# Stores of left and right output columns: from POOL's queue and whole row groups to SyncE's queue and row halves

## The chip, the cores and the metric

The kernel runs on one core of a Trainium2 chip. The metric is the device time of one execution in microseconds (us), the median of the runs; less is better.

## The reference

Two stages, the second fed by the first. Attention: batch 4, 8 heads, 768 positions, head size 64. Heads flagged as retrieval heads look back over all positions, the others over the first 4 positions and a window of 64. The result is laid out as `x` with 3072 rows and 512 columns. Then a soft mixture of experts with 8 experts and 4 slots for each:

```python
logits = x @ phi                      # 3072 x 32
slot_input = softmax over rows (logits).T @ x       # 32 x 512
for e in range(8):                    # 4 slots each
    h = relu(slot_input[e] @ w1[e])   # 512 -> 1024
    slot_out[e] = h @ w2[e]           # 1024 -> 512
out = softmax over slots (logits) @ slot_out        # 3072 x 512, float32
```

The output is 6.29 MB in float32. The weights `w1` and `w2` are 16.8 MB each in float32 and are stored as bf16 on the chip.

## The kernel before

A planner (`Plan`) takes a list of operations with costs and keys and writes out an order for all engines before the program is built; the key decides among operations that could start. `pl.op` adds one.

All weights but one half are loaded by POOL's queue (`dma`, line 347), one after the other, over the whole run. The last experts' `w2` comes in column halves: experts 6 and 7 (`NSPLIT = 2`), left 256 columns first, then the right 256 columns. `load_half(15, 1)` is the last load; it lands in `qk`.

The end of the kernel, which the change touches, goes like this. `w2_op` (line 1046) multiplies one expert's hidden rows by its `w2`, in the left columns (`c = 0`) and then the right ones (`c = 1`). Between the last two experts of each half stands `wait_zeros` (ops `ZT0` and `ZT1`, line 1064): multiplications of a tile of zeros, on PE, whose results nobody reads. `emit_so` (line 1104) scales the half of the slot outputs.

The output rows are six groups of 512 rows (`gi` 0 to 5); a group is a tile of 128 partitions with four rows `r` each. `out_tile` (lines 1121, 1129, 1131) multiplies one row `r` of a group by the slot outputs on PE, and ACT or DVE scale it into the group's buffer. Groups 0 to 2 (`NL = 12` rows, the list `halved`) are done in two passes, left 256 columns and right 256 columns, so that the left pass can go ahead of the last weight half. Groups 3 to 5 are done in full rows after it.

`store` (line 1140) writes rows `r0` to `r1` of a group to the output, from POOL's queue or from SyncE's. It waits for the scaling of these rows. Left stores: group 0 in rows 0 and 1 to 3, groups 1 and 2 whole, all from POOL. Right stores: group 0 in rows 0 to 1 and 2 to 3, groups 1 and 2 whole, all from SyncE. Full rows: three stores of 1 MB from SyncE. SyncE's queue also carries three loads at the program's start (lines 475 to 477), so that it issues ten transfers. A queue's instructions are issued in order; each one's wait holds up those behind it. Each transfer has a semaphore out of eight per kind of queue, so that from the ninth on it also waits for the landing of the one eight before it.

Of the kernel before, what the change touches and what calls it, by code (L numbers as in the profile page):

```python
# [151 lines left out]
def pe(ns, n=1):  # L152
    occ = ns * n / 1000.0
    return {"PE": (occ, occ + 0.27)}
# [72 lines left out]
def kernel(  # L227
# [101 lines left out]
    def on(eng, occ, late=0.18):  # L329
        return {eng: (occ, occ + late)}  # L330
# [349 lines left out]
    for b in range(B):  # L680
# [57 lines left out]
        for ns in ([(0, 1), (2, 3)] if b == 0 else [(0, 1, 2, 3)]):  # L738
# [10 lines left out]
            def emit_ex2(o, b=b, sc=sc, ns=ns):  # L749
# [4 lines left out]
            e = pl.op(f"EXX.{b}.{ns[0]}", on("ACT", 0.12 + 0.213 * len(ns)), key - 1.0, deps=[a, PTXb[b].op],  # L754
                      acq=[PTXb[b]] if ns[0] == 0 else [], rel=[sc], emit=emit_ex2)

            def emit_mx(o, b=b, ns=ns):
# [4 lines left out]
            e = pl.op(f"MX.{b}.{ns[0]}", on("DVE", 0.07 + 0.134 * len(ns)), key + 0.3, deps=[e] + [o_hm[n] for n in ns],  # L762
                      emit=emit_mx)
# [209 lines left out]
    kt = T * 16 + 10  # L973
# [65 lines left out]
    w2o = {}  # L1039

    def w2_op(e, c0, c1):
        def emit_w2(o):
            e4, g0 = e // 4, e % 4
            for fo in range(8):
                g = fo % 4
                nc.tensor.matmul(banks[so.slot][32 * g:32 * (g + 1), 256 * c0:256 * c1],
                                 hT_t[e4][:, fo, 32 * g0:32 * (g0 + 1)], w_row(NE + e, fo) if c1 - c0 == 2 else w_half(NE + e, c0)[:, fo, :],
                                 start=(e == 0 and fo < 4), stop=(e == NE - 1 and fo >= 4),
                                 tile_position=(0, 32 * g), skip_group_check=True)

        land = [wland[NE + e]] if c1 - c0 == 2 else [hland[NE + e, c0]]
        o = pl.op(f"W2.{e}" + ("" if c1 - c0 == 2 else f".{c0}"), on("PE", 0.22 * (c1 - c0), 0.27),
                  kt + (29 + e if c0 == 1 else 16 + e),
                  deps=[hte[e // 4]] + land + [w2o[c] for c in range(c0, c1) if c in w2o],
                  acq=[so] if e == 0 else [], emit=emit_w2, mode="c32", mm=8)
        for c in range(c0, c1):
            w2o[c] = o
# [3 lines left out]
    def wait_zeros(name, n, key, dep, first=False):  # L1061
        def emit_z(o):
            for _ in range(n):
                nc.tensor.matmul(banks[zw.slot][:, 0:448], ident, zt, start=True, stop=True)

        pl.op(name, pe(190, n), key, deps=[dep], acq=[zw] if first else [], rel=[zw], emit=emit_z, mode="full", mm=n)
# [4 lines left out]
    for c in range(2):  # L1071
        for e in range(NE - NSPLIT, NE):
            w2_op(e, c, c + 1)
            if e == NE - 2:
                wait_zeros(f"ZT{c}", 3, kt + (29.5 + e if c else 22.5), w2o[c], c == 0)

    def out_lhs(gi, r):
        return expT[:, r, 128 * gi:128 * (gi + 1)]
# [32 lines left out]
    def ot_view(gi):  # L1111
        return slots[wbuf[gi].slot][:, 0:8 * KB].bitcast(F32).rearrange("p (r d) -> p r d", r=4)
# [3 lines left out]
    def out_tile(m, gi, r, c0, c1, key):  # L1116
        bf, w = Buf("BK"), 256 * (c1 - c0)
        cs = slice(256 * c0, 256 * c1)

        def emit_om(o):  # L1120
            nc.tensor.matmul(banks[bf.slot][:, 0:w], out_lhs(gi, r), slot_out[:, cs], start=True, stop=True)  # L1121

        a = pl.op(f"OM.{gi}.{r}.{c0}", on("PE", 0.06 + w / 2400.0, 0.27), key, deps=so_e[c0:c1], acq=[bf],
                  emit=emit_om, mode="full", mm=1)

        def emit_oe(o):
            d, sc_ = ot_view(gi)[:, r, cs], rrow[:, 4 * gi + r:4 * gi + r + 1]
            if o.eng == "ACT":
                nc.scalar.activation(d, banks[bf.slot][:, 0:w], ACT.Copy, scale=sc_)  # L1129
            else:  # L1130
                nc.vector.tensor_scalar(d, banks[bf.slot][:, 0:w], sc_, None, op0=ALU.mult)  # L1131

        x, y = (0.24 + w / 1070.0, 0.13 + w / 960.0)
        oe[m, gi, r] = pl.op(f"OE.{gi}.{r}.{c0}", {"ACT": (x, x + 0.19), "DVE": (y, y + 0.17)}, key, deps=[a, o_rw[gi]],
                             rel=[bf], emit=emit_oe)

    def store(eng, m, gi, r0, r1, cs, key):
        def emit_st(o):
            dst = out[512 * gi:512 * (gi + 1), :].rearrange("(p r) d -> p r d", r=4)
            (nc.gpsimd if eng == "POOL" else nc.sync).dma_start(dst[:, r0:r1, cs], ot_view(gi)[:, r0:r1, cs])  # L1140

        pl.op(f"ST.{m}.{gi}.{r0}", on(eng, 0.7), key, deps=[oe[m, gi, r] for r in range(r0, r1)], emit=emit_st)

    NL = 12
    halved = [(gi, min(4, NL - 4 * gi)) for gi in range((NL + 3) // 4)]
    for gi, n in halved:
        for r in range(n):
            out_tile("l", gi, r, 0, 1, kt + 30 + 0.1 * (4 * gi + r))
    for gi, r0, r1 in [(0, 0, 1), (0, 1, 4)] + [(gi, 0, n) for gi, n in halved[1:]]:
        store("POOL", "l", gi, r0, r1, slice(0, 256), kt + 31 + gi + 0.1 * r0)  # L1150
    for gi, n in halved:
        for r in range(n):
            out_tile("r", gi, r, 1, 2, kt + 40 + 0.1 * (4 * gi + r))
        for r0, r1 in [(0, 2), (2, 4)] if gi == 0 else [(0, n)]:
            store("SP", "r", gi, r0, r1, slice(256, 512), kt + 41 + gi + 0.1 * r0)
    for gi in range(6):
        n = dict(halved).get(gi, 0)
# [55 lines left out]
```

## Time and profile before

| | |
|---|---|
| median of 3 runs | 148.62 us (148.15 to 148.8) |
| the profiled execution | 148.91 us, span 147.1 us |
| granted TensorE clock, mean | 0.968 |
| busy share of the span | PE 81%, DVE 75%, ACT 73%, POOL 29% |
| DMA packets | 33.40 MB, mean 227 GB/s |
| read from HBM, written to it | 52.49 MB, 6.29 MB |

Times in the profile count from the span's start. A row of the timeline is start, length, engine, line, operation, and what is written and read; an "x2" merges two neighbours. A row of a DMA window gives a queue's packets, its MB and the share of 16 engines' time that its packets took; packets may overlap, so that a share can be above one. `q0 software_dynamic` holds what POOL issues, `q1 hardware_dynamic` what SyncE issues. Loads that convert float32 to bf16 count by what they write, half of what they read.

### The profile page before, as it was taken

To read this page: it belongs to the slowest core of one execution; us is meant where nothing else is said; L and a number is where in the kernel's file an instruction comes from. 1 tells how busy PE (TensorE), PEld (TensorE's weight loads), DVE (VectorE), ACT (ScalarE), POOL (GpSimd) and SP (SyncE) were. 2 spreads that over 40 slices of the span, in tenths; PEclk is the share of its full clock that TensorE was granted. 3 is DMA by queue.
4 is the path that set the end of the run, shared out by engine and by line. 5 is a ranking of instruction groups with operands and counts; after the bars stand their busy time and mean duration, and the time that the engine had idled before them with its cause. 6 is when DMAs were issued, how large, how long until landed. Compare 5 with 4: busy or idle time off the path is not lost.

```text
span 147.1 us, 4879 instructions
## 1 busy us (share of the span) xinstructions
PE 119.7 (81%) x2107; PEld 79.2 (54%) x2107; DVE 111.0 (75%) x254; ACT 107.9 (73%) x147; POOL 42.0 (29%) x75
## 2 busy tenths in 40 slices
PE   0167988999989999999999999999959899879000
PEld 0045666677776657776558766666745445443000
DVE  1786299999999999999799899999973312549500
ACT  3152689999999997999998999999971460649200
POOL 6988631120311380100170011405380000340000
PEclk9999999999999999999999999999995999999965
DMA  5999999999999999999999999999999999989995
GB/s 147 270 207 212 217 213 214 213 215 211 216 215 214 212 215 214 217 214 214 215 215 217 214 215 214 214 214 215 214 214 214 206 196 197 168 309 347 404 423 212
DMA packets 13815, 33.40 MB, mean 227 GB/s; under 512 B 802, under 2 KB 6562, under 8 KB 13282
## 3 DMA queue, kind: packets, MB, share of 16 engines
q0 software_dynamic: 11472, 27.27, 94.1%
q1 hardware_dynamic: 2322, 5.83, 10.5%
q8 instruction: 16, 0.26, 0.6%
q14 instruction: 5, 0.04, 0.1%
HBM read 52.49 MB, written 6.29 MB: 400 GB/s over the span
## 4 chain that ended last, share of the span: by engine, by line
PE 27%; DVE 26%; DMA 18%; ACT 15%; issue 5%; POOL 1%; SPq 0%; DVEq 0%; ACTq 0%; POOLq 0%
DMA qk<-in_moe_w_dram 14%; ACT pt L726 11%; PE sc L656 6%; DVE pt L672 5%; PE pv L800 5%; DVE xv L824 5%; DMA phf<-in_moe_phi_dram 4%; DVE qk L336 4%; PE tr L604 3%; PE tr L630 3%; PE bk L1121 2%; PE tr L863 2%; DVE xv L336 2%; DVE slot L1131 2%; DVE vf L705 2%
## 5 line engine op out<-in xcount | busy, mean ns | idle before, releaser
L726 ACT ACTIVATE pt<-sc 128x1024 bf16<-128x1024 f32 x80 | 77.0, 1047 | 3.0 <-PE sc L656 2.8
L656 PE MATMUL sc<-qk 64*128 64x512 bf16 (+3 forms) x256 | 31.4, 311 | 1.2 <-ACT pt L726 0.8
L672 DVE TENSOR_TENSOR pt<-pt,msk 128x1024 bf16<-128x1024 bf16 (+1 forms) x48 | 29.0, 610 | 2.0 <-ACT pt L726 1.8
L800 PEld LDWEIGHTS <-pt 128*128 128x128 bf16 x640 | 23.4, 98 | 6.2 <-issue 5.2
L800 PE MATMUL pv<-vx,pt 128*128 128x65 bf16 x320 | 25.6, 193 | 0.3 <-DVE xv L824 0.2
L800 PE MATMUL pv<-vf,pt 128*128 128x65 bf16 x320 | 21.3, 195 | 0.9 <-DVE xv L824 0.9
L347 POOL DMA_DIRECT2D slot<-in_moe_w_dram x11 | 7.7, 696 | 40.0 <-PE tr L630 34.3
L336 DVE COPY qk<-tr 128x768 bf16<-128x768 bf16 (+2 forms) x33 | 15.1, 482 | 2.1 <-PE tr L604 1.8
L630 PE MATMUL tr<-ident,slot 128*64 128x128 bf16 (+1 forms) x448 | 16.3, 219 | 0.4 <-ACT qk L334 0.3
L824 DVE TENSOR_TENSOR xv<-pv,rs 128x768 bf16<-128x768 f32 (+1 forms) x17 | 15.5, 911 | 0.6
L630 PEld LDWEIGHTS <-slot 128*64 128x64 bf16 (+1 forms) x448 | 13.1, 109 | 5.1 <-issue 4.8
L656 PEld LDWEIGHTS <-qk 64*128 64x128 bf16 x256 | 10.4, 94 | 9.6 <-issue 3.3
L887 POOL COPY expT<-eT 128x192 bf16<-128x192 bf16 x12 | 7.4, 667 | 12.5 <-ACT eT L870 12.5
L1131 DVE TENSOR_SCALAR slot<-bk,rrow 128x256 f32<-128x256 f32 (+1 forms) x19 | 9.2, 562 | 2.2 <-PE bk L1121 2.2
L336 DVE COPY xv<-tr 128x512 bf16<-128x512 bf16 (+2 forms) x20 | 8.0, 410 | 2.5 <-PE tr L604 2.2
L836 PE MATMUL tr<-ident,xv 128*128 128x128 bf16 x96 | 8.4, 224 | 1.3 <-DVE xv L824 0.9
L604 PEld LDWEIGHTS <-slot 96*64 96x64 bf16 x192 | 6.8, 141 | 4.3 <-issue 4.0
L604 PE MATMUL tr<-ident_u,slot 96*64 96x96 bf16 x192 | 7.9, 248 | 1.6 <-DVE phi L544 1.1
L336 DVE COPY xT<-tr 128x768 bf16<-128x768 bf16 (+1 forms) x14 | 7.5, 539 | 1.1 <-PE tr L836 1.1
L1129 ACT ACTIVATE slot<-bk,rrow 128x256 f32<-128x256 f32 (+1 forms) x17 | 7.7, 570 | 0.9 <-PE bk L1121 0.9
L690 PE MATMUL tr<-ident,xv 128*128 128x128 bf16 x96 | 8.1, 220 | 0.0
L1140 POOL DMA_DIRECT2D out_dram<-slot x4 | 2.9, 714 | 17.7 <-DVE slot L1131 17.6
(121 smaller groups left out, 165.6 us busy)
## 6 DMA issues: line engine op xcount, KB each, us to landing
slot<-in_moe_w_dram POOLq DMA_DIRECT2D x10, 1024.0 KB, 24.6
out_dram<-slot SPq DMA_DIRECT2D x3, 1024.0 KB, 5.9
slot<-in_q_dram POOLq DMA_DIRECT2D x2, 768.0 KB, 19.9
slot<-in_k_dram POOLq DMA_DIRECT2D x2, 768.0 KB, 23.8
qk<-in_moe_w_dram SPq DMA_DIRECT2D x1, 1024.0 KB, 6.3
slot<-in_v_dram POOLq DMA_DIRECT2D x2, 512.0 KB, 21.5
qk<-in_moe_w_dram POOLq DMA_DIRECT2D x1, 1024.0 KB, 17.4
vx<-in_moe_w_dram POOLq DMA_DIRECT2D x1, 1024.0 KB, 21.5
```

The source lines that it names most:

```text
L336: nc.vector.tensor_copy(dst, src)
L347: acq=[buf] if buf else [], lead=1.3, emit=lambda o: nc.gpsimd.dma_start(dst(), src))
L604: nc.tensor.transpose(t[64 * i:64 * (i + 1), :, :, s, :], rv[:, i, 8 * c + s, :], ident_u)
L630: nc.tensor.transpose(t[64 * i:64 * (i + 1), :, s, :], rv[:, i, 8 * c + s, :], ident[0:R, 0:R])
L656: nc.tensor.matmul(scb[sc.slot][:, i, c:c + 128 * nb], kk, qq.rearrange("p b c -> p (b c)"), start=True, stop=True)
L672: nc.vector.tensor_tensor(pT, pT, mh, op=ALU.mult)
L690: nc.tensor.transpose(t[:, 128 * j:128 * (j + 1)], vT[:, 6 * n + j, :], ident)
L726: nc.scalar.activation(pTs[PTb[b, n].slot][:, :, 512 * g:512 * (g + 1)], scb[sc.slot], ACT.Exp, scale=scale)
L800: nc.tensor.matmul(pvb[:, bk, c:c + 65], lt, rhs, start=(j == 0), stop=(j == i))
L824: nc.vector.tensor_tensor(xo, pvw[:, :, :, 0:64], r.rearrange("p i (j o) -> p i j o", o=1).to_broadcast([P, 2, i1 - i0, 64]), op=ALU.mult)
L836: nc.tensor.transpose(t[:, 128 * i:128 * (i + 1)], xv[:, i, 128 * n:128 * (n + 1)], ident)
L1131: nc.vector.tensor_scalar(d, banks[bf.slot][:, 0:w], sc_, None, op0=ALU.mult)
```

## The change

The left stores of groups 1 and 2 move from POOL's queue to SyncE's, and each becomes two stores of two rows. The right stores of groups 1 and 2 also become two stores of two rows each. SyncE issues sixteen transfers instead of ten. The left stores come ahead of the right ones on that queue. Group 0's stores and the full rows are as before. `ZT1`, the zeros ahead of the right half's last expert, has two multiplications instead of three; `ZT0` keeps three.

```diff
@@ weights w2, by halves @@
             if e == NE - 2:
-                wait_zeros(f"ZT{c}", 3, kt + (29.5 + e if c else 22.5), w2o[c], c == 0)
+                wait_zeros(f"ZT{c}", 2 if c else 3, kt + (29.5 + e if c else 22.5), w2o[c], c == 0)
@@ stores @@
-    for gi, r0, r1 in [(0, 0, 1), (0, 1, 4)] + [(gi, 0, n) for gi, n in halved[1:]]:
-        store("POOL", "l", gi, r0, r1, slice(0, 256), kt + 31 + gi + 0.1 * r0)
+    for gi, r0, r1 in [(0, 0, 1), (0, 1, 4)] + [(gi, x, x + 2) for gi, n in halved[1:] for x in (0, 2)]:
+        store("SP" if gi else "POOL", "l", gi, r0, r1, slice(0, 256), kt + 31 + gi + 0.1 * r0)
     for gi, n in halved:
         for r in range(n):
             out_tile("r", gi, r, 1, 2, kt + 40 + 0.1 * (4 * gi + r))
-        for r0, r1 in [(0, 2), (2, 4)] if gi == 0 else [(0, n)]:
+        for r0, r1 in [(0, 2), (2, 4)]:
             store("SP", "r", gi, r0, r1, slice(256, 512), kt + 41 + gi + 0.1 * r0)
```

## The prediction

> **What bounds the kernel now.** I read the page first, for the span and the DMA rows.
>
> ```profile
> span 147.1 us, 4879 instructions
> DMA  5999999999999999999999999999999999989995
> q0 software_dynamic: 11472, 27.27, 94.1%
> q1 hardware_dynamic: 2322, 5.83, 10.5%
> ```
>
> The DMA engines are busy in nearly every slice, to the last one. Transfers issued by POOL run on q0, those issued by SyncE on q1. Next I read the stretch that the change touches, with the table of busy time by stretch (columns: PE, PEld, DVE, ACT, POOL, granted clock, DMA share, GB/s).
>
> ```profile
> 120.00:125.00 5.00, 5.00 (x90) 2.40 (x83) 1.31 (x3) 0.69 (x1) 0.00 (x0) 1.00 1.45 195
> 127.50:128.00 0.50, 0.47 (x4) 0.28 (x3) 0.50 (x2) 0.50 (x3) 0.45 (x1) 1.00 0.72 93
> 129.00:129.50 0.50, 0.30 (x2) 0.09 (x1) 0.04 (x1) 0.00 (x1) 0.50 (x1) 1.00 0.40 127
> 129.50:130.00 0.50, 0.00 (x0) 0.00 (x0) 0.00 (x0) 0.00 (x0) 0.49 (x2) 1.00 0.96 334
> 130.50:131.00 0.50, 0.43 (x16) 0.36 (x13) 0.03 (x1) 0.41 (x1) 0.00 (x0) 1.00 0.66 246
> 131.00:131.50 0.50, 0.38 (x4) 0.34 (x4) 0.28 (x2) 0.07 (x1) 0.00 (x0) 1.00 1.00 393
> ```
>
> From 131.0 us on the DMA engines are full and stores are all that runs on them; before that lie two thin places, 129.0 to 129.5 (share 0.40) and 130.5 to 131.0 (0.66). Then the chain of waits, from 108.94 on (start, length, what), which says when the right half can begin:
>
> ```profile
> 108.94 21.16 DMA qk<-in_moe_w_dram
> 130.15 0.43 PE bk L1046 x8
> 130.59 0.48 ACT msk L1104
> 131.12 1.61 PE bk L1121 x12
> ```
>
> The last weight half lands at 130.10 (108.94 + 21.16), and only then can the right columns be multiplied and scaled. Last, the timeline of POOL and of SyncE's queue shows where the stores are issued (start, length):
>
> ```profile
> 127.37 0.58 POOL L1140 DMA_DIRECT2D out_dram<-slot  x1 [17.56 <-DVE slot L1131]
> 128.05 0.76 POOL L1140 DMA_DIRECT2D out_dram<-slot  x1
> 128.81 1.52 POOL L1140 DMA_DIRECT2D out_dram<-slot  x2
> 132.09 0.41 SPq L1140 DMA_DIRECT2D out_dram<-slot  x1
> 132.60 0.45 SPq L1140 DMA_DIRECT2D out_dram<-slot  x1
> 133.54 0.62 SPq L1140 DMA_DIRECT2D out_dram<-slot  x1
> 134.32 0.53 SPq L1140 DMA_DIRECT2D out_dram<-slot  x1
> 135.65 0.35 SPq L1140 DMA_DIRECT2D out_dram<-slot  x1
> ```
>
> So the question about the end is what the slowest DMA engine still has to move. The DMA windows (packets, MB, share of 16 engines) answer it:
>
> ```profile
> DMA packets 6, 0.00 MB, mean 12 GB/s; under 512 B 0, under 2 KB 6, under 8 KB 6
> q0 software_dynamic: 6, 0.00, 9.0%
> DMA packets 69, 0.27 MB, mean 338 GB/s; under 512 B 2, under 2 KB 3, under 8 KB 69
> q0 software_dynamic: 29, 0.12, 97.1%
> q1 hardware_dynamic: 54, 0.06, 74.4%
> q0 software_dynamic: 17, 0.00, 8.6%
> ```
>
> The first two rows are 129.10 to 129.35: six packets, a share of 9.0%. While all engines read weights the share was 1.45 (row 120 to 125), so 9.0% is 0.062 of that, one engine in sixteen: fifteen engines stand idle and one still reads the last weight half. The third row is 129.7 to 130.5, where one data packet under 2 KB is left (two of the three are semaphore writes under 512 B): that engine reads until about 129.7. The fourth row is 133.15 to 133.50, stores of q0 alone; the last two are 133.50 to 133.74, where q1 takes over as q0 runs out, the last engine near 133.7.
>
> **The change part by part.** Same bytes, same packets of rows; different queue, size and issue time. The rates come from three windows: q0 stores at 131.0 to 133.4, the two half stores of right group 0 on q1 at 133.74 to 135.1, the whole stores of right groups 1 and 2 on q1 at 135.25 to 137.75.
>
> ```profile
> DMA packets 241, 0.92 MB, mean 382 GB/s; under 512 B 17, under 2 KB 17, under 8 KB 241
> DMA packets 486, 0.47 MB, mean 348 GB/s; under 512 B 24, under 2 KB 486, under 8 KB 486
> DMA packets 934, 0.94 MB, mean 376 GB/s; under 512 B 16, under 2 KB 934, under 8 KB 934
> ```
>
> Left groups 1 and 2, 1.049 MB: at q0's 382 GB/s they take 2.75 us. As four halves on q1 no row shows them on the left, but the right halves of group 0 have the very shape: at 348 GB/s 3.01 us, +0.27. The other bound is the rate of whole q1 stores, 376 GB/s: 2.79 us, +0.04.
>
> Right groups 1 and 2, again 1.049 MB: now 2.79 us at 376 GB/s, as halves 3.01 us at 348, +0.22; the other bound is 0. Together +0.04 to +0.49. The rows that are nearest, same queue and same shape, stand at the upper end; but that window begins while q0 is only just empty and some of its slowness may be that, so I take +0.4.
>
> The gaps. With POOL, left groups 1 and 2 are issued at 128.81 and after it, since one issue takes about 0.76 us of the engine. The scaling shows when the rows were ready:
>
> ```profile
> 127.00 2.04 DVE L1131 TENSOR_SCALAR slot<-bk,rrow 128x256 f32<-128x256 f32 x5
> 127.07 1.93 ACT L1129 ACTIVATE slot<-bk,rrow 128x256 f32<-128x256 f32 x5
> ```
>
> The engines take turns on rows, a pair every 0.39 us, and the last two pairs are group 2's, ending near 128.65 and 129.04; group 1's end near 127.91 and 128.27. SyncE can then issue at about 128.05, 128.5, 129.0 and 129.5 instead of 128.81 and 129.57. The delay from an issue on SyncE to its first packet is seen at the program's start:
>
> ```profile
> 0.73 0.38 SPq L475 DMA_DIRECT2D qk<-in_moe_w_dram  x1
> DMA packets 0, 0.00 MB, mean 0 GB/s; under 512 B 0, under 2 KB 0, under 8 KB 0
> q1 hardware_dynamic: 9, 0.07, 150.0%
> ```
>
> No packet from 0.73 to 1.75, nine from 1.7 to 2.0: about 1.03 us. The left halves reach the engines from 129.1 on and the thin places fill up. For fifteen engines the left half ends earlier, but the right half can't begin before 132.09 + 1.03 = 133.12, where it now begins at 133.50: at most 0.38 us. For the sixteenth there is nothing to fill. It has read until 129.7 and then owes 98 KB of left stores (a sixteenth of 1.573 MB); at 382/16 = 23.9 GB/s that is 4.1 us, which ends at 133.8, where q0 does run out. It has no idle time now, so it ends no earlier. That these two are the same engine I infer from the sum, as no view numbers the engines. The kernel waits for the last engine, so I take 0 for the gaps and keep -0.38 as the bound.
>
> Issues on SyncE: six more of 0.41 to 0.62 us each. Four lie between 128.05 and 130, when its queue is empty until 132.09. Two more lie between 132.60 and 135.65: at 0.5 us apiece the six of the right side end near 135.1, before the whole rows are ready at 135.65. The last half of group 2 goes out at about 134.65, 0.33 us later than the whole at 134.32, but it stands behind five halves of 0.75 us that begin near 133.8, so its turn comes after 137. Nothing waits behind it. POOL loses two issues and has no work after them. Each store from SyncE's ninth transfer on waits for the landing of the one eight before; the tightest is the first right half of group 2, behind a left half that is over 2 us old. All this is free as long as the stores queue at the engines; without that cover the 0.33 us would show.
>
> One zero multiplication less in ZT1:
>
> ```profile
> 128.56 0.74 PE L1064 MATMUL bk<-zt,ident 128*128 128x448 bf16 x3
> 130.15 0.40 PE L1046 MATMUL bk<-qk,xT 128*32 128x256 bf16 x8 [0.84 <-DMA qk<-in_moe_w_dram]
> ```
>
> PE then idles about 1.04 us before the last weight half instead of 0.84; the wait is for the DMA, so 0. If the granted clock fell to half for it, the right matmuls (12 in 1.61 us by the chain, 0.13 a row) would take 0.27 us a row against 0.20 for DVE and ACT together (two rows every 0.39 us), and the first right store would come some 0.3 us later, at 133.4 on the engines and so inside the last one's backlog: 0 again.
>
> The Trainium skill's page "DMA: Bandwidth & Descriptors" (Rules for kernel authors) speaks against cutting transfers: coalesce small ones, and two halves of one transfer only run one after the other on the same engines. Its fit (Anatomy of one DMA) is 2.0 us fixed plus bytes, so six more transfers would cost 12 us if they ran strictly one by one; the rows above, a mean of 348 against 376 GB/s, show the fixed part overlapped and only a twelfth of the rate lost.
>
> **Sum.** 0.27 + 0.22, taken as +0.4, gaps 0, rest 0. The profiled execution took 148.91 us, 0.29 above the median of 148.62. 148.91 + 0.4 = 149.31 in its terms, 149.0 us against the median. Its own range is 148.7 to 149.2.
>
> **Rivals.** First, the gaps pay. If it is not one engine that sets the end, but all sixteen in turn, the right half starts 0.38 us earlier and the halves run at 376 GB/s: 148.62 - 0.38 + 0.04 = 148.3 us. For it speaks the empty row of 129.10 to 129.35; against it the sum that leads the slow engine to 133.8.
>
> Second, slower: the left halves push the last weight half back. They reach the slow engine near 129.1, when it has some 17 weight packets left (six in 0.25 us until 129.7). Now q0 keeps stores behind weights; on q1 they may be taken in turns. A 1 KB store packet takes 47 ns of an engine (348/16 = 21.8 GB/s). One per weight packet delays the landing by 0.8 us, and the right half comes at 133.9 instead of 133.12, still behind the left stores, which end near 134 on that engine: free. From two per weight packet on it decides: 1.6 us, the right half comes at 134.7, some 0.7 us after the slow engine ran dry, with the halves' 0.49: 148.62 + 1.2 = 149.8 us. Against it speaks the only other place where both queues hold work, 4.95 to 5.25:
>
> ```profile
> q1 hardware_dynamic: 70, 0.05, 52.1%
> q0 software_dynamic: 8, 0.02, 44.5%
> ```
>
> There q0 begins as q1 empties, and at 133.5 q1 begins as q0 empties although the store had been issued 1.4 us before: both look like one queue run out before the other is taken, though neither proves it. The same page (Queues, rings and completion order) says otherwise: each engine goes round between the queues, packet groups of some 9 to 17 descriptors at a time. By that rule this rival holds.
>
> Third, the cut transfers cost nothing at 376 GB/s and the gaps nothing either: 148.7, inside the forecast's range. That the edits are not made can be left out: the four left halves and four right ones stand on SyncE's queue in the changed program.
>
> **How the numbers follow.** About 0.5%, 0.74 us, is what a measurement of this kernel can tell from no change, so 147.88 and 149.36 are the borders. Forecast 0.5, of which 0.09 spills over 149.36 (all the upper costs and a little more); gaps pay 0.2, of which 0.05 falls below 147.88; weights pushed back 0.2, slower; something not seen 0.1, of which 0.02 faster, 0.06 slower. Faster 0.07, same 0.58, slower 0.35. The range goes from the first rival's 148.3 less 0.1 to the second's 149.8 plus 0.2.
>
> **What would show it.** Right: q1 packets from about 129.1 on, the window at 129.2 no longer empty, the last weight half still landing near 130.1, the right stores' rate near 348 GB/s throughout, the whole rows' stores ending some 0.4 us later. Wrong: a landing of the last weight half beyond 130.8, or q1 empty at 133 to 134 (second rival); the last store ending before 145.2 (first rival).

## Result: 0.36% faster, and most of it after the last store

| | before | after |
|---|---|---|
| median, 22 runs each | 148.43 us | 147.81 us |
| lowest to highest | 147.75 to 148.95 | 147.30 to 148.44 |
| ratio, 95% interval | | 0.9964 (0.9949 to 0.9978) |
| profiled execution, span | 148.91, 147.1 | 148.12, 146.3 |

The change gains 0.36% of 148.43, 0.53 us by the ratio; the medians themselves lie 0.62 us apart. The gain is inside the 0.5% that the prediction called no change, but the interval excludes 1, the sign is against the +0.4 us that was forecast, and 147.81 lies below the forecast's own range (148.7 to 149.2) and below that of all rivals together (148.2 to 150.0). The kernel before took 148.43 us here instead of the 148.62 that the prediction started from, so that 0.2 us of the distance is its starting point.

The profile after, the rows that answer to those of before. First the table of busy time by stretch (PE, PEld, DVE, ACT, POOL, granted clock, DMA share, GB/s):

```profile
129.00:129.50 0.50, 0.18 (x5) 0.17 (x8) 0.03 (x1) 0.00 (x0) 0.00 (x0) 1.00 1.01 354
130.50:131.00 0.50, 0.50 (x6) 0.45 (x5) 0.29 (x1) 0.18 (x1) 0.00 (x0) 1.00 1.06 371
131.00:131.50 0.50, 0.50 (x6) 0.43 (x5) 0.50 (x2) 0.50 (x2) 0.00 (x0) 1.00 0.92 311
```

The two thin places of before (shares 0.40 and 0.66) are full in this execution. Then the timeline of SyncE's queue and of PE, and the chain:

```profile
127.94 0.40 SPq L1140 DMA_DIRECT2D out_dram<-slot  x1
128.44 0.45 SPq L1140 DMA_DIRECT2D out_dram<-slot  x1
128.99 0.45 SPq L1140 DMA_DIRECT2D out_dram<-slot  x1
129.53 0.45 SPq L1140 DMA_DIRECT2D out_dram<-slot  x1
129.43 0.40 PE L1046 MATMUL bk<-qk,xT 128*32 128x256 bf16 x8 [0.32 <-DMA qk<-in_moe_w_dram]
109.49 19.89 DMA qk<-in_moe_w_dram
```

The four left halves go out as early as was said. The last weight half lands at 129.38 (109.49 + 19.89) instead of 130.10, and PE waits only 0.32 us for it. Whether the change did that is a question for the experiments.

The row that matters most stands behind the last store. These are SyncE's own instructions from the last DMA packet to the end, in the view of line 1208 (count, shortest/median/longest ns, first and last start); before first, after second:

```profile
L1208 SPq EVENT_SEMAPHORE  x9: 17/28/28, 145.8 to 147.0; - x9
```

```profile
L1208 SPq EVENT_SEMAPHORE  x3: 17/17/28, 145.4 to 146.2; - x3
```

At its end the program waits for every DMA semaphore in a fixed row; in the trace one instruction starts some 0.06 us after the other. The semaphores of SyncE's transfers are taken in turn, eight of them. In both views the first instruction is the wait for the last store itself, and the last two belong to the closing barrier. With ten transfers the last store has the second semaphore: when it lands, six more instructions follow whose semaphores are long there. With sixteen transfers the last store has the eighth, and nothing follows but the barrier. From the last packet to the end of the span, the tail, the kernel before takes 1.62 us (145.48 to 147.10), the changed one 1.27 (145.04 to 146.31).

### The profile page after: what moved, and what is told of

Read it like the earlier page. It is cut to its first block, busy times and chain, and to the rows that moved or that the text cites. A ratio compares the mean times of both kernels' runs of the same rounds, so it can differ in the third digit from the quotient of the medians.

```text
span 146.3 us, 4885 instructions
## 1 busy us (share of the span) xinstructions
PE 120.2 (82%) x2106; PEld 79.2 (54%) x2106; DVE 110.5 (76%) x254; ACT 108.2 (74%) x147; POOL 40.4 (28%) x73
## 4 chain that ended last, share of the span: by engine, by line
PE 31%; DVE 26%; DMA 18%; ACT 12%; issue 5%; POOL 1%; SPq 0%; DVEq 0%; ACTq 0%; POOLq 0%
DMA qk<-in_moe_w_dram 14%; ACT pt L726 9%; PE sc L656 7%; DVE pt L672 5%; PE pv L800 5%; DVE xv L824 5%; PE tr L604 5%; DMA phf<-in_moe_phi_dram 4%; DVE qk L336 3%; PE tr L630 3%; PE bk L1121 3%; PE tr L690 2%; DVE xv L336 2%; PE tr L863 2%; PE tr L836 2%
## 5 line engine op out<-in xcount | busy, mean ns | idle before, releaser
L836 PE MATMUL tr<-ident,xv 128*128 128x128 bf16 x96 | 8.3, 219 | 1.7 <-DVE xv L824 0.9
L690 PE MATMUL tr<-ident,xv 128*128 128x128 bf16 x96 | 8.8, 232 | 0.0
L836 PEld LDWEIGHTS <-xv 128*128 128x128 bf16 x96 | 5.9, 97 | 3.2 <-DVE xv L824 1.8
```

What stands on the lines that cost most here:

```text
L690: nc.tensor.transpose(t[:, 128 * j:128 * (j + 1)], vT[:, 6 * n + j, :], ident)
L836: nc.tensor.transpose(t[:, 128 * i:128 * (i + 1)], xv[:, i, 128 * n:128 * (n + 1)], ident)
```

## Experiments

Theory 1: the six waits at the program's end, the exit, are most of the gain, 0.35 us. Theory 2: most of it comes from the stores, by filled gaps. Spare loads of 64 bytes at the program's start set the count of SyncE's transfers without touching a store.

**The exit alone, three times.** The kernel before and

```diff
-        nc.sync.dma_start(phf, ...)
+        nc.sync.dma_start(phf, ...); [nc.sync.dma_start(spare[:, x_, :], ri_src) for x_ in range(6)]
```

> The kernel before, with six loads of 64 bytes more at the start of SyncE's queue into a spare tile, so that it issues sixteen transfers, the stores as before. Theory 1 (the exit): the last store's semaphore is then the last of the row of waits at the end instead of the third, and the six waits of 0.06 us behind it are already passed; 0.37 us less, ratio 0.9975 to the kernel before, and the profile's tail from the last landing to the end 0.87 us instead of 1.23. Theory 2 (the stores): the gain of the change comes from filled gaps and earlier stores, which this kernel doesn't have; ratio 1.000.

> The kernel before with six small loads once more, for the size of the stores' own part beside the next one: 0.9975 by the exit's waits alone.

> The kernel before with six small loads: the exit's waits alone, 0.35 us, ratio 0.9976.

Measured: 0.9975 (0.9961 to 0.9990), 0.9993 (0.9967 to 1.0018), 0.9963 (0.9938 to 0.9987); the mean is 0.9977, 0.34 us. The second interval alone doesn't exclude 1. The end of the first, in the same view:

```profile
L1208 SPq EVENT_SEMAPHORE  x3: 17/17/28, 145.3 to 146.1; - x3
```

Three instructions as in the changed kernel; the tail is 1.26 to 1.27 us in the three traces. (The expectations' 1.23 and 0.87 us count from the end of the wait for the last store, 0.38 to 0.40 us behind the last packet; the difference is the same.) Six loads that nobody reads are worth over half of the change.

**Halfway.** The same with `range(3)`, so that the last store has the fifth semaphore.

> The kernel before with three small loads: thirteen transfers, the last store's semaphore in the middle of the row. Theory 1: three waits are left behind the last landing instead of six or none, the tail from the last packet to the end halfway between 1.62 and 1.27 us, 1.44. If the tail does not go by this row, it stays at 1.62.

```profile
L1208 SPq EVENT_SEMAPHORE  x6: 17/28/28, 144.6 to 145.6; - x6
```

Six instructions, a tail of 1.45 us, against 1.62 with nine and 1.27 with three: 0.06 us for each wait that stands behind the last landing. Its single time, 147.47 us, says nothing by itself. Over all fourteen kept traces the tail goes by the count of transfers alone: 1.61 to 1.62 us with ten or eighteen (three traces), 1.45 with thirteen, 1.25 to 1.27 with sixteen (ten traces), whatever the stores are.

**The changed kernel without the exit's gain, twice.** The change and `range(2)`: eighteen transfers, the last store has the second semaphore again.

> The changed kernel with two loads of 64 bytes more at the start of SyncE's queue, so that the last store takes the same semaphore as in the kernel before. Theory 1 (the exit): the six waits come back, 0.37 us more than the changed kernel; what is left is the stores' own part, ratio about 0.9989 to the kernel before, tail 1.23 us. Theory 2 (the stores): the ratio stays at 0.9964.

> The changed kernel with two small loads, so that its last store has the same semaphore as in the kernel before: what differs from the kernel before is the stores' own part alone. If that part is about 0.18 us, as the runs so far have it, ratio 0.9988; if there is none, 1.000.

Measured: 0.9981 (0.9963 to 1.0000) and 0.9988 (0.9961 to 1.0016). Its end is that of before:

```profile
L1208 SPq EVENT_SEMAPHORE  x9: 17/28/28, 145.3 to 146.5; - x9
```

The tail is 1.62 us. So the stores' own part, the gain that doesn't come from the exit, is what is left, 0.0015 on the mean or 0.2 us, and neither interval by itself proves it.

**The change itself once more.**

> The changed kernel itself on the same chip: exit's waits 0.35 us and stores' own part 0.18 us, ratio 0.9964.

0.9965 (0.9941 to 0.9990), as the first time.

**Left move alone, right halves alone.** Each with spare loads up to sixteen transfers and three multiplications in `ZT1`. The left move alone, twice (right groups 1 and 2 whole):

```diff
-        for r0, r1 in [(0, 2), (2, 4)]:
+        for r0, r1 in [(0, 2), (2, 4)] if gi == 0 else [(0, n)]:
```

> The left move alone, in halves on SyncE; right groups whole, three multiplications in ZT1, two small loads so that SyncE issues sixteen transfers. Theory 1: the exit's 0.37 us and the stores' own part, ratio about 0.9964. Theory 2: the left move carries all, 0.9964 too. By the term of the prediction that right halves cost 0.22 us it would be 0.995; if they cost nothing, 0.9964.

> The left move alone at sixteen transfers once more. If the stores' own part is real, the ratio is 0.0010 to 0.0015 below that of the kernel before with six small loads; if it is chance, the two agree.

The right halves alone (left stores as before):

> Right halves alone, left stores whole from POOL, three multiplications in ZT1, four small loads so that SyncE issues sixteen transfers. Theory 1: the exit's 0.37 us, ratio 0.9975 if right halves cost nothing, 0.999 if they cost the predicted 0.22 us. Theory 2: 1.000 or a little above, as the gaps stay.

Measured: left move 0.9967 (0.9951 to 0.9982) and 0.9949 (0.9928 to 0.9970), right halves 0.9979 (0.9961 to 0.9997). The left move alone gives all that the change gives; the right halves stand with the exit alone, so that no gain or cost of theirs shows. The DMA windows of right groups 1 and 2 say the same; first the right halves alone at 135.1 to 137.0, then whole groups (six spare loads) at 134.7 to 137.1:

```profile
DMA packets 747, 0.72 MB, mean 380 GB/s; under 512 B 42, under 2 KB 747, under 8 KB 747
```

```profile
DMA packets 902, 0.91 MB, mean 378 GB/s; under 512 B 16, under 2 KB 902, under 8 KB 902
```

380 against 378 GB/s: cutting these stores in two cost no rate.

All kernels at sixteen transfers with left halves on SyncE (the change twice, the left move twice) have 0.9964, 0.9965, 0.9967 and 0.9949, mean 0.9961; with POOL's left stores (six spare loads, three times) 0.9977. The difference, 0.0016 or 0.24 us, agrees with the 0.0015 at eighteen transfers against ten. Both comparisons point to a store part of about 0.2 us, but they average over chips. On one and the same chip, the kernels with SyncE's left stores lie below the one with six spare loads by 0.0008, by 0.0044, and once above it by 0.0002 (the change itself, 0.9965 against 0.9963), so that the mean leans on one pair. An estimate from all single times (least squares with one mean for each chip, the kernel of the next section left out) gives -0.35 us for the exit and -0.16 for the stores, give or take 0.11 each, if the executions are independent of each other. The exit's part is shown; the stores' part is likely, and its size is not.

**All left stores on SyncE.** From the kernel before, with no spare load needed for sixteen transfers:

```diff
-    for gi, r0, r1 in [(0, 0, 1), (0, 1, 4)] + [(gi, 0, n) for gi, n in halved[1:]]:
-        store("POOL", "l", ...)
+    for gi, r0, r1 in [(gi, x, x + 2) for gi, n in halved for x in (0, 2)]:
+        store("SP", "l", ...)
```

> All left stores on SyncE in halves, group 0's too, right groups 1 and 2 whole, three multiplications in ZT1: sixteen transfers without any spare load. The first store is issued near 127.2 instead of 127.94 and its packets reach engines that have finished the weights, but also those that still read. Theory 1 (exit 0.37 us, the rest from filled gaps): ratio 0.9955 to 0.997. Rival: packets of the two queues taken in turns, as the changed kernel's trace shows at 130 to 131, push the last weight half back by 0.4 to 0.9 us and the right half with it; ratio 0.998 or more.

> All left stores on SyncE in halves, right groups 1 and 2 whole. If filling more of the engines' idle time before the weights land is worth anything beyond the changed kernel, the ratio is below 0.9964 by 0.0005 to 0.001; if the DMA engines then only wait for the right half, as its first trace shows near 131, it equals the changed kernel's.

Measured: 0.9943 (0.9921 to 0.9966) and 0.9963 (0.9940 to 0.9987). It beats the kernel before. The second equals the changed kernel's 0.9965 on the same chip; the first is lower, on a chip where the changed kernel didn't run and the left move alone has 0.9949. Whether it is better than the change stays open. What it shows of the queues is clear. Its DMA window at 127.5 to 128.5, while the last weight half is being read:

```profile
q0 software_dynamic: 191, 0.10, 70.7%
q1 hardware_dynamic: 193, 0.19, 54.9%
```

In that 1.0 us 191 packets of weights pass beside 193 of stores; the kernel before passed 206 in the 1.1 us from 127.4 to 128.5, with no store beside them. So here the stores on SyncE's queue take room that the weights leave, and the weights go on at their rate. Then, at 131 to 132:

```profile
131.00:131.50 0.50, 0.50 (x4) 0.38 (x3) 0.50 (x2) 0.47 (x2) 0.00 (x0) 0.50 0.65 225
131.50:132.00 0.50, 0.50 (x4) 0.35 (x3) 0.50 (x2) 0.36 (x1) 0.00 (x0) 0.50 0.57 203
```

the left half is stored so early that the engines wait for the right half (shares 0.65 and 0.57): part of the filled gap opens again later. The granted clock is 0.50 in this execution; at 1.00, in the second trace, the share at 131.5 to 132.0 is still down to 0.78.

**Is the earlier landing of the weights part of it?** No run was made for that, but the kept traces tell much of it. The chain's row before the last weights' multiplication, in the kernel before with six spare loads (second run), with three, and in the changed kernel with two (second run):

```profile
108.24 20.89 DMA qk<-in_moe_w_dram
```

```profile
107.68 21.40 DMA qk<-in_moe_w_dram
```

```profile
108.15 22.20 DMA qk<-in_moe_w_dram
```

Landings at 129.13 and 129.07 with POOL's stores, 130.35 with SyncE's, beside 130.10 before and 129.38 after. The landing goes up and down by 1.3 us from execution to execution, and its mean is the same, 129.6 in the six traces with POOL's left stores and 129.5 in the eight with SyncE's: it doesn't go with the change. So the 0.72 us by which it is earlier in the profiled pair is chance as far as these traces show, and so is some of the 0.44 us by which the last packet is earlier there.

The traces also tell when the stores can matter. Take the time from PE's first multiplication with the last weight half to the last DMA packet. In ten of the fourteen traces it is 14.9 to 15.2 us, in five with POOL's left stores and in five with SyncE's. There the landing sets the end, and the queue of the left stores makes no difference. The changed kernel's second trace is one of them (130.09 to 145.21), and in it the engines run thin again before the right half comes:

```profile
132.50:133.00 0.50, 0.49 (x3) 0.11 (x2) 0.50 (x3) 0.50 (x3) 0.00 (x0) 1.00 0.35 123
```

In the other four traces that time is longer: 15.3 us in the kernel before, 15.6 to 15.8 in three with SyncE's stores, whose weights landed only 1.6 to 2.0 us after POOL's first left store was issued. From that issue to the last packet it is 18.1 us in the kernel before and 17.6 to 17.7 in those three. So where the left stores set the end, SyncE's way is some 0.45 us shorter; where the landing does, it gains nothing, and a mean of 0.2 us lies between. This is an argument from traces, with one of POOL's against three of SyncE's; no run holds the landing still.

## Why the prediction was wrong

**The step that is missing: the exit.** The part on SyncE's issues says that each store from the ninth transfer on waits for the one eight before, and stops there. The same row of semaphores is waited for once more at the end, and it is the count of transfers, ten or sixteen, that decides how much of it is left after the last landing. The spare loads show this term at -0.35 us in the trace and -0.34 in the times. With it, the prediction's +0.4 would have been about zero; that the time fell by 0.5 us takes the next two terms as well. The case that came stood under "something not seen", with a chance of 0.1.

**"As halves on q1 at 348 GB/s": the term that was mis-sized.** The sum took +0.4 us from the two half stores of group 0. The right halves, priced at +0.22, measured nothing: 380 GB/s, and the ratio of the exit alone. So the shape was not the cause of 348. The rate goes by the time. In the changed kernel q1's left halves have, at 131.5 to 132.0 and at 132.2 to 134.5:

```profile
DMA packets 203, 0.19 MB, mean 383 GB/s; under 512 B 16, under 2 KB 203, under 8 KB 203
DMA packets 817, 0.79 MB, mean 342 GB/s; under 512 B 48, under 2 KB 817, under 8 KB 817
```

and in the kernel before q0's whole left stores have, at 131 to 132 and at 132.2 to 133.4:

```profile
DMA packets 103, 0.41 MB, mean 414 GB/s; under 512 B 2, under 2 KB 2, under 8 KB 103
DMA packets 105, 0.43 MB, mean 355 GB/s; under 512 B 1, under 2 KB 1, under 8 KB 105
```

In these two traces either queue falls by over a tenth at 132, with wholes and with halves. A window of another time was taken for a window of another shape. What makes this stretch slower no run here separates; it lies in the time when the right half is multiplied and scaled.

The left halves are another matter. "Same packets of rows" doesn't hold for them: POOL's left stores go out in packets of 4 KB (0.41 MB in 103), SyncE's in packets of 1 KB (0.19 MB in 203). At like times q1 stands below q0, 383 against 414 and 342 against 355 GB/s. On the 1.049 MB of left groups 1 and 2 that is 0.1 to 0.2 us, an estimate from these four rows, so that part of the +0.27 may be real and is inside the stores' part above. No run separates it.

**"Gaps: 0, since the sixteenth engine sets the end".** The thin places are filled, and the stores' part is about -0.2 us by the means, between the 0 that was taken and the bound of -0.38. The slow engine is there in some executions and not in others: at 129.10 to 129.35 the changed kernel's trace has

```profile
q1 hardware_dynamic: 80, 0.08, 94.8%
q0 software_dynamic: 6, 0.01, 8.8%
```

and the six packets of q0 are two stores of 4 KB and four semaphores, as the last weight packet ended at 129.0. In its last 0.75 us of weights the kernel before read 19 packets, and so did two later traces with SyncE's stores (the change's second, the second with two spare loads); the changed kernel's first trace read 109. A bound on all executions can't rest on an engine that is late in some of them. The first rival, that gaps pay, fits the traces, with about half of its price.

**The second rival** didn't come. The landing was not pushed back, by the means above, and in the two traces of the kernel that stores earliest it came at 129.1 and 129.5. Its premise was right all the same. At 130.2 to 130.9 of the changed kernel's trace both queues hold stores:

```profile
q0 software_dynamic: 50, 0.20, 81.7%
q1 hardware_dynamic: 48, 0.05, 19.0%
```

50 packets of 4 KB beside 48 of 1 KB: here the engines take the queues in turns, packet for packet. The prediction took two hand-overs for signs that one queue runs out before the other is taken; that was wrong. The Trainium skill's page "DMA: Bandwidth & Descriptors" (Queues, rings and completion order) says that each engine goes round between the queues, a whole packet at a time. The trace agrees, 50 packets against 48. The two rules of the same page of the Trainium skill (Rules for kernel authors) that the prediction holds against cut transfers speak of transfers under 64 KB and of halves by partitions, and its fit (Anatomy of one DMA) is given for the path of POOL's transfers. The halves here are of rows, 256 KB each and issued by SyncE, and on the right they cost no rate: 380 against 378 GB/s.

**What held.** No cost of SyncE's six more issues shows, and the left halves reached the engines at 128.9, as the rows of before had said. One multiplication less in `ZT1` moved nothing that shows in the times: the left move alone keeps three and is as fast. But the 0 rested on a wait of 0.84 us for the weights, and this wait goes with the landing. In the second trace of the left move there is none:

```profile
128.79 0.74 PE L1064 MATMUL bk<-zt,ident 128*128 128x448 bf16 x3
129.46 0.40 PE L1046 MATMUL bk<-qk,xT 128*32 128x256 bf16 x8
```

The weights had landed at 129.23, and three multiplications held PE until 129.46.

## What to carry to other kernels

Follow the sum past the last store: read what the issuing queue still does after the last landing, and count transfers modulo the number of semaphores before calling a few tenths of a microsecond an effect of the stores. When two rows differ in shape and in time, look for a row of the same shape at another time before a price is put on the shape. A single late engine or landing in one trace is not a bound; compare it over several executions first, and ask of each trace which of two paths ended last.

## What was not expected of the hardware

A wait on a semaphore that is already there took 0.06 us of SyncE's queue, so that six of them are 0.24% of this kernel. While the last weights were read with a share of 0.71 (0.73 with no store beside them), the engines took 0.19 MB of stores in 1.0 us from the other queue with no loss to the weights. Where two queues had work they were served packet for packet, so that the queue with 4 KB packets got 0.20 MB where the one with 1 KB packets got 0.05.
